# A fused Sinkhorn-attention and feed-forward kernel: a rearranged front, Sinkhorn rounds on GpSimd, and another order of the loads

## The chip, the cores and the metric

The kernel runs on one core of a Trainium2 chip. The metric is device time in microseconds (us) of one execution. A profiled execution is also shown: its span, and who was busy and who waited in it.

## The reference, cut to what matters

Four batches of eight heads, 768 tokens and 64 channels go through an attention whose keys and values are first mixed between eight blocks of 96 tokens. The mixing matrix P comes from five rounds of exponential, row and column normalisation (Sinkhorn). A squared-ReLU feed-forward layer follows.

```python
P = sort_net                                    # (4, 8, 8, 8)
for _ in range(5):
    P = P - np.max(P, axis=-1, keepdims=True)
    P = np.exp(P)
    P = P / (np.sum(P, axis=-1, keepdims=True) + 1e-09)
    P = P / (np.sum(P, axis=-2, keepdims=True) + 1e-09)
k_sorted = np.einsum('bhij,bhjcd->bhicd', P, k_b)   # k, v in 8 blocks of 96 tokens
v_sorted = np.einsum('bhij,bhjcd->bhicd', P, v_b)
scores = scale * np.matmul(q_b, k_sb.transpose(0, 1, 2, 4, 3))   # block i against sorted block i
attn = softmax(scores);  x = np.matmul(attn, v_sb)   # then (3072, 512), heads side by side
h = x @ w_in                                    # 512 x 2048
r = np.maximum(h, 0.0)
out = (s * (r * r) + b) @ w_out                 # 2048 x 512
```

## The kernel before, in words

The order of the instructions on every engine is that of the program text; nothing is rescheduled, and each engine takes its instructions in order. TensorE (PE) does all products and the transposes of batches 0 and 1; VectorE (DVE) and ScalarE (ACT) empty PSUM and do the small arithmetic; GpSimd (POOL) issues the converting loads of q, k, v, `w_in` and `w_out` and rearranges v; SyncE (SP) loads `sort_net` and the f32 values of batch 0, stores the output and issues DMA transposes.

**Front (L76 to L299).** Batch 0 has a Sinkhorn of its own on 128 partitions. The first round comes from an exponential (L240), a product (L250) and a reciprocal (L254). Four rounds follow (loop at L266): an exponential on ACT, a product `rs` on PE, then on DVE a reciprocal, a product with a row sum, and a reciprocal. In every round `permute0` (L209) casts a quarter of the values `v0f`, half on ACT and half on DVE. Between these stand products with zeros, `warm(n, w, m)` (L126), in rounds 0 and 1 `warm(50, 16, 64)`. `pd0` (L258) makes the mixing operand from the last round. POOL meanwhile issues half of the queries, k, all of `w_in`, the other queries and `w_out` (L146 to L166), without waiting for anything but its eight DMA semaphores, each of which must have come back before it is used again.

**First half of batch 0 (L541 to L567).** `kh` and `vh` are 32 small products per piece with `PD0` and an evacuation (A is ACT, D is DVE). `s_piece` makes scores and their exponential, `p_piece` the attention times values and its normalisation on DVE, `t_piece` transposes, `part` begins the first feed-forward product `hps` (L490).

**Feed-forward.** `ffn1(t, slots)` (L494) runs eight pairs of 128 columns of `w_in`; each ends in a ReLU `rt` on ACT (L502) and a square `gt` on DVE (L503), and then in the work that its slot holds. `ffn2(t, slots)` (L508) has a slot after every four products `ops` (L514). There are two of each per batch, t = 2b and 2b + 1. The work on the next batch is in the slots.

**Sinkhorn of batches 1 to 3.** `sink(it)` (L333) does a round on 32 partitions: exponential on ACT, the rest on DVE. Rounds 0, 1, 2 are in slots 3, 5, 7 of `ffn1(1)`, rounds 3 and 4 in slots 0 and 1 of `ffn2(0)`. In slot 2 `build_pd(1)` (L351) takes the result to PE (`pe`, L353) and makes batch 1's mixing operand. `make_bias` (L603, slot 4 of `ffn1(1)`) makes `bias` out of `w_out` with 16 products, four DVE steps, and three copies on POOL (L615). In `ffn2(0)` slots 4, 7 and 9 then hold the keys (`k_piece`), queries (`q_half`) and values (`v_piece`) of batch 1. PSUM is had from two pools, `psa` with three buffers and `psb` with two.

POOL's queue after the front is, in order: memsets, the loads of batch 1, `v_sort(1)` (eight copies, L207), the loads of batch 2, the bias copies, the loads of batch 3, `v_sort(2)` and `v_sort(3)`.

Of the kernel before, what the change touches and what calls it, by code (L numbers as in the profile page):

```python
# [22 lines left out]
def kernel(  # L23
# [49 lines left out]
    CQ = S // 2 // 128  # L73
# [27 lines left out]
    def load_qh(b, half, hs):  # L101
        if b not in QH:
            QH[b] = rawp.tile([128, 2, H, CQ, D], BF, tag="rawq", name="qh")
        qv = q[b].rearrange("h (f p c) d -> f p h (c d)", f=2, c=CQ)
        nc.gpsimd.dma_start(out=QH[b][:, half, hs].rearrange("p h c d -> p h (c d)"),
                            in_=qv[half][:, hs])
# [17 lines left out]
    nc.vector.memset(VP[0][:, :, C2:GAP], 0.0)  # L124

# [20 lines left out]
    load_qh(0, 0, slice(0, 4))  # L146
    load("k", 0, 3)
    load_qh(0, 0, slice(4, 8))
    fill_vs(0)
    load_wi(0, 512, slice(0, 2))  # L150
    load_wi(0, 512, slice(2, 4))
    load_wi(512, 1024)
    load_qh(0, 1, slice(0, 8))
    load_wi(1024, 1536)
    load_wi(1536, 2048)
# [6 lines left out]
    for t, src in ((s_bc, moe_s), (b_bc, moe_b)):  # L162
        nc.gpsimd.dma_start(out=t, in_=src.to_broadcast([128, 1]))
    for c in range(4):
        fs = slice(c * (NF // 4), (c + 1) * (NF // 4))
        nc.gpsimd.dma_start(out=wo[:, fs, :], in_=wov[:, fs, :])  # L166
# [12 lines left out]
    er = const.tile([128, NB], FP)  # L179
    er2 = const.tile([128, NB, 2], FP)  # L180
    bmx = const.tile([128, 2 * NHP, HB, 2], FP)
    ex = const.tile([128, NB], FP)
    rr = const.tile([128, NB], FP)
    csum = const.tile([128, 1], FP)
    crec = const.tile([128, 1], FP)
# [8 lines left out]
                            axis=AX.X, op=ALU.add)  # L194
    nc.vector.tensor_scalar(out=hs64, in0=hs64, scalar1=2.0, scalar2=None, op0=ALU.mult)
    nc.vector.tensor_reduce(out=hsel, in_=ident.rearrange("p (h g) -> p h g", h=H),
                            axis=AX.X, op=ALU.add)
    nc.vector.tensor_reduce(out=nmax, in_=s0, axis=AX.X, op=ALU.max, negate=True)
# [17 lines left out]
    def q_trans(b, half, hp0):  # L216
        if b not in QT:
            QT[b] = trp.tile([128, 2, NHP, CQ, 128], BF, tag="qt", name="qt")
        tr = psb.tile([128, 1024], BF, tag="b", name="tq")
        for a in range(2):  # L220
            for c in range(CQ):
                for e in range(2):
                    o = (a * CQ + c) * 128
                    nc.tensor.transpose(out=tr[e * 64:(e + 1) * 64, o:o + 128],
                                        in_=QH[b][:, half, 2 * (hp0 + a) + e, c, :],
                                        identity=ident)
        return tr

    def q_piece(b, half, hp0, eng):
        tr = q_trans(b, half, hp0)  # L230
        evac(eng, QT[b][:, half, hp0:hp0 + 2],
             tr[:, 0:2 * CQ * 128].rearrange("p (a c t) -> p a c t", a=2, c=CQ))
# [14 lines left out]
    warm(5)  # L247
    warm(16, 16, 64)
# [5 lines left out]
    nc.vector.reciprocal(out=crec, in_=e0[:, 0, NB:NB + 1])  # L254
    src = e0[:, 0, 0:NB]
    PD0 = [const.tile([128, 2, NHP, HB, 2], BF, name=f"pdh{i}") for i in range(2)]
# [8 lines left out]

    for it in range(4):  # L266
        nc.scalar.activation(out=ex, in_=src, func=AF.Exp, scale=crec)
        permute0(it)
        if it == 0:
            nc.vector.tensor_reduce(  # L270
                out=bm.rearrange("p (e a z) -> p e a z", e=2, z=2),
                in_=idv.rearrange("p a e j z -> p e a z j"), axis=AX.X, op=ALU.add)
            nc.vector.tensor_scalar(
                out=bmx, in0=bm.rearrange("p (g z) -> p g z", z=2).unsqueeze(2)
                .broadcast_to([128, 2 * NHP, HB, 2]), scalar1=2.0, scalar2=None, op0=ALU.mult)
# [3 lines left out]
        if it == 3:  # L279
            q_piece(0, 0, 0, "A")  # L280
            warm(2)
        elif it == 2:
            warm(3)
        else:
            warm(50, 16, 64)
        nc.vector.reciprocal(out=rr, in_=rs[:, 0, 0:NB])
        if it < 3:
            nc.vector.scalar_tensor_tensor(out=er, in0=ex, scalar=1.0, in1=rr, op0=ALU.mult,
                                           op1=ALU.mult, accum_out=csum)
        else:  # L290
            nc.vector.scalar_tensor_tensor(
                out=er2, in0=ex.unsqueeze(2).broadcast_to([128, NB, 2]), scalar=1.0,
                in1=rr.unsqueeze(2).broadcast_to([128, NB, 2]), op0=ALU.mult, op1=ALU.mult,
                accum_out=csum)
        nc.vector.reciprocal(out=crec, in_=csum)
        src = er
        if it == 1:
            nc.vector.memset(KS[0][:, :, :, C2:GAP], 0.0)
# [33 lines left out]
    def sink(it):  # L332
        if it == 0:  # L333
            nc.vector.tensor_reduce(out=rstat, in_=sn, axis=AX.X, op=ALU.max)
            nc.vector.tensor_tensor(out=sn, in0=sn, in1=rstat.broadcast_to([BH, NB, NB]),
                                    op=ALU.subtract)
        nc.scalar.activation(out=sn, in_=sn, func=AF.Exp)
        nc.vector.tensor_reduce(out=rstat, in_=sn, axis=AX.X, op=ALU.add)
        nc.vector.reciprocal(out=rrec, in_=rstat)
        nc.vector.tensor_tensor(out=sn, in0=sn, in1=rrec.broadcast_to([BH, NB, NB]), op=ALU.mult)  # L340
        if it == 4:
            return
        nc.vector.tensor_reduce(out=rstat, in_=sn.rearrange("p i j -> p j i"),
                                axis=AX.X, op=ALU.add)
        if it == 0:
            nc.vector.tensor_tensor(out=rstat, in0=rstat, in1=eps, op=ALU.add)
        nc.vector.reciprocal(out=rrec, in_=rstat)
        nc.vector.tensor_tensor(out=sn, in0=sn, in1=spread(rrec, [[0, NB], list(rrec.ap[1])]),
                                op=ALU.mult)
# [21 lines left out]
    def q_half(b, half, eng):  # L371
        if b not in QT:
            QT[b] = trp.tile([128, 2, NHP, CQ, 128], BF, tag="qt", name="qt")
        tr = psa.tile([128, 2, 1024], BF, tag="a", name="tqa")
        for a in range(NHP):
            for c in range(CQ):
                for e in range(2):
                    o = (a % 2 * CQ + c) * 128
                    nc.tensor.transpose(out=tr[e * 64:(e + 1) * 64, a // 2, o:o + 128],
                                        in_=QH[b][:, half, 2 * a + e, c, :], identity=ident)  # L380
        evac(eng, QT[b][:, half].rearrange("p (u a) c t -> p u (a c t)", u=2),
             tr[:, :, 0:2 * CQ * 128])
# [24 lines left out]
    def s_piece(b, half, hp):  # L407
# [3 lines left out]
        for n in range(HB):  # L411
            for e in range(2):
                pr = slice(e * 64, (e + 1) * 64)
                if byp:
                    o = sc[:, e, 0:TG].rearrange("p (c t) -> p c t", c=CQ)[:, :, 32 * n:32 * n + 32]
                    r = QT[b][pr, half, hp, :, 32 * n:32 * n + 32]
# [123 lines left out]

    kh(0, 0, "A", psa)  # L541
    kh(0, 1, "D", psa)
    pd0(1)
    kh(0, 2, "A", psa)
    vh(0, 0, "D", psb)
    vh(0, 1, "A", psb)
    vh(0, 2, "D", psa)
    s_piece(0, 0, 0)
    vh(0, 3, "D", psa)
    q_piece(0, 0, 2, "A")  # L550
    s_piece(0, 0, 1)
    warm(1)
    p_piece(0, 0, 0)
    warm(1)
    p_piece(0, 0, 1)
    t_piece(0, 0, 0, "A")
    s_piece(0, 0, 2)
    part(0, 0, (0,))
    t_piece(0, 0, 1, "D")
    s_piece(0, 0, 3)  # L560
# [3 lines left out]
    p_piece(0, 0, 3)  # L564
    part(0, 1, (0, 1))
    t_piece(0, 0, 2, "A")
# [3 lines left out]
    nc.gpsimd.memset(ones, 1.0)  # L570
    nc.gpsimd.memset(VP[1][:, :, C2:GAP], 0.0)
    nc.gpsimd.memset(KS[1][:, :, :, C2:GAP], 0.0)
    eps = const.tile([BH, NB], FP)
    nc.gpsimd.memset(eps, 1e-9)
    fill_vs(1)
    load("v", 1)
    load("k", 1)
    for half in range(2):
        load_qh(1, half, slice(0, 8))

    def v_sort(b):
        for i in range(8):
            permute(nc.gpsimd, b, RAW["v", b], ds=slice(i * 8, (i + 1) * 8))

    v_sort(1)
    for t in "kv":
        load(t, 2)
    load_q_rows(2)


    rstat = const.tile([BH, NB], FP)
    rrec = const.tile([BH, NB], FP)
# [26 lines left out]
    def QP(hp, eng): return lambda: q_piece(0, 1, hp, eng)  # L619
    def QF(b, half, eng): return lambda: q_half(b, half, eng)  # L620
    def SK(it): return lambda: sink(it)
# [10 lines left out]
    def halves(n, more=()):  # L632

        if n == 1:
            s0 = {0: [SK(3)], 1: [SK(4)], 2: [PDB(1)],
                  4: [K(n, 0, "D"), K(n, 1, "A"), K(n, 2, "D")],
                  7: [QF(n, 0, "D"), QF(n, 1, "A")],
                  9: [V(n, 0, "D"), V(n, 1, "A"), V(n, 2, "D")]}
# [3 lines left out]
        s1 = {0: [V(n, 3, "D"), SC(n, 0, 0), SC(n, 0, 1)],  # L642
# [4 lines left out]
        for i, p in more:  # L647
# [3 lines left out]
    ffn1(0, {0: [KH(1, "D")], 1: [KH(2, "A"), QP(0, "D")],  # L651
             2: [VH(0, "D"), VH(1, "A")], 3: [SC(0, 1, 0), VH(2, "D")],
             4: [VH(3, "D"), SC(0, 1, 1)], 5: [P(0, 1, 0), QP(2, "D")],
             6: [SC(0, 1, 2), P(0, 1, 1), TP(0, 1, 0, "A")],
             7: [SC(0, 1, 3), P(0, 1, 2), TP(0, 1, 1, "D")]}, {0: 2, 1: 2})
# [5 lines left out]
    ffn1(1, {2: [make_sel], 3: [SK(0)], 4: [make_bias], 5: [SK(1)], 7: [SK(2)]}, {0: 2, 1: 2})  # L661
    s0, s1 = halves(1, [(5, LD("k", 3)), (6, LD("v", 3)), (7, lambda: load_q_rows(3))])
# [45 lines left out]
```

## Time and profile before

| | us |
|---|---|
| median of three runs (252.92 to 257.52) | 255.03 |
| the profiled execution | 254.47 |
| its span | 252.3 |
| PE busy in the span | 232.4 (92%) |
| DVE, ACT, POOL busy | 128.7, 97.1, 57.8 |
| first feed-forward product `hps` | at 30.00 |
| `ffn1(1)` runs on from | 57.16 |
| `pe`, PE's product for batch 1's mixing operand | at 75.50 |

Busy time is the time in which an engine executes. A wait is named by the instruction that waits and by the one that released it. The chain of work is followed back from the last instruction: it shows at each moment what the end waited for. In all rows "L" is a line of the kernel before. The granted clock is a record of changes of TensorE's clock; before the first recorded change it is shown as full. The shapes and durations of the products tell more there.

### The profile page before, as it was taken

To read this page: it belongs to the slowest core of one execution; us is meant where nothing else is said; L and a number is where in the kernel's file an instruction comes from. 1 tells how busy PE (TensorE), PEld (TensorE's weight loads), DVE (VectorE), ACT (ScalarE), POOL (GpSimd) and SP (SyncE) were. 2 spreads that over 40 slices of the span, in tenths; PEclk is the share of its full clock that TensorE was granted. 3 is DMA by queue.
4 is the path that set the end of the run, shared out by engine and by line. 5 is a ranking of instruction groups with operands and counts; after the bars stand their busy time and mean duration, and the time that the engine had idled before them with its cause. 6 is when DMAs were issued, how large, how long until landed. Compare 5 with 4: busy or idle time off the path is not lost.

```text
span 252.3 us, 6386 instructions
## 1 busy us (share of the span) xinstructions
PE 232.4 (92%) x2810; PEld 141.6 (56%) x2832; DVE 128.7 (51%) x273; ACT 97.1 (38%) x131; POOL 57.8 (23%) x86
## 2 busy tenths in 40 slices
PE   6997899879919999999999999999999999999994
PEld 3956666545505655565665565656555656664453
DVE  4433454655975479654463566444545674442221
ACT  3433554545511242456640334566403336661000
POOL 8565400992130469900000000000000000000000
PEclk9999999999976999999999999999999999999999
DMA  6999999969901899772001113720021133000122
GB/s 154 263 202 205 152 213 212 151 111 188 85 0 44 159 191 154 107 183 49 0 3 74 53 44 107 191 38 3 3 83 44 44 104 107 0 1 20 65 83 84
DMA packets 42332, 25.07 MB, mean 99 GB/s; under 512 B 33344, under 2 KB 37696, under 8 KB 42304
## 3 DMA queue, kind: packets, MB, share of 16 engines
q0 software_dynamic: 22320, 12.85, 36.6%
q1 hardware_dynamic: 19984, 11.81, 16.6%
q8 instruction: 22, 0.36, 0.6%
q14 instruction: 6, 0.05, 0.1%
HBM read 27.27 MB, written 6.29 MB: 133 GB/s over the span
## 4 chain that ended last, share of the span: by engine, by line
PE 84%; DVE 8%; ACT 3%; issue 3%; DMA 1%; DVEq 0%; ACTq 0%
PE ops L514 31%; PE hps L490 30%; PE pv L442 3%; PE sc L420 3%; PE z L129 3%; PE tv L398 3%; PE vh L323 2%; PE tp L388 2%; DVE gt L503 2%; PE ops L527 1%; PE kh L309 1%; ACT rt L502 1%; DVE x L448 1%; DVE bias L612 1%; PE rs L277 1%
## 5 line engine op out<-in xcount | busy, mean ns | idle before, releaser
L490 PE MATMUL hps<-xt,wi 128*128 128x384 bf16 x512 | 86.6, 326 | 2.5 <-DVE xt L238 1.8
L514 PE MATMUL ops<-wo,gt 128*128 128x512 bf16 x347 | 83.4, 385 | 2.2 <-issue 1.6
L490 PEld LDWEIGHTS <-wi 128*128 128x128 bf16 x512 | 49.1, 98 | 34.8 <-issue 3.3
L502 ACT ACTIVATE rt<-hps 128x768 bf16<-128x768 f32 x64 | 51.7, 810 | 40.4 <-PE hps L490 40.4
L503 DVE TENSOR_TENSOR gt<-rt 128x768 bf16<-128x768 bf16 x64 | 35.9, 561 | 47.4 <-ACT rt L502 47.2
L514 PEld LDWEIGHTS <-gt 128*128 128x128 bf16 x368 | 33.9, 99 | 37.5 <-issue 1.7
L535 DVE SCALAR_TENSOR_TENSOR ot<-ops,s_bc,bias 128x512 f32<-128x512 f32 (+1 forms) x25 | 18.2, 729 | 33.7 <-PE ops L514 31.4
L207 POOL COPY vp<-rawv 128x384 bf16<-128x384 bf16 x24 | 20.1, 888 | 13.0 <-DMA rawv<-in_v_dram 13.0
L448 DVE TENSOR_TENSOR x<-pv,rec 96x512 bf16<-96x512 f32 x32 | 22.0, 687 | 1.1
L428 ACT ACTIVATE at<-sc 112x768 bf16<-112x768 f32 x16 | 12.1, 806 | 21.0 <-PE sc L420 21.0
L424 ACT ACTIVATE at<-sc 112x768 bf16<-112x768 f32 x16 | 12.5, 808 | 12.3 <-PE sc L420 12.3
L442 PEld LDWEIGHTS <-at 112*128 112x128 bf16 (+1 forms) x256 | 13.1, 103 | 7.0 <-ACT at L428 0.6
L116 POOL DMA_DIRECT2D qtok<-in_q_dram x16 | 12.3, 778 | 10.2 <-DMA rawv<-in_v_dram 5.2
L442 PE MATMUL pv<-vs,at 112*128 112x66 bf16 (+1 forms) x256 | 14.3, 198 | 0.0
L238 DVE CAST vs<-tv 112x1024 bf16<-112x1024 f32 x9 | 10.7, 1221 | 5.9 <-PE tv L398 5.9
L129 PE MATMUL z<-zeros 128*64 128x16 bf16 (+1 forms) x127 | 12.4, 238 | 1.4 <-DVE zeros L120 1.2
L447 DVE RECIPROCAL rec<-pv 96x8 f32<-96x8 f32 x32 | 6.4, 201 | 9.4 <-PE pv L442 9.3
L420 PE MATMUL sc<-qt,ks 64*128 64x96 bf16 x256 | 9.2, 208 | 0.9 <-DVE qt L238 0.9
L129 PEld LDWEIGHTS <-zeros 128*64 128x64 bf16 (+1 forms) x128 | 7.9, 155 | 3.5 <-issue 2.1
L236 ACT CAST vs<-tv 112x1024 bf16<-112x1024 f32 x3 | 3.1, 1018 | 16.8 <-PE tv L398 16.8
L323 PE MATMUL vh<-pdh,vp 128*64 128x32 bf16 x256 | 6.7, 199 | 1.8 <-issue 1.8
L238 DVE CAST ks<-tp 128x1024 bf16<-128x1024 f32 x6 | 7.1, 1220 | 1.8 <-PE tp L388 1.6
(108 smaller groups left out, 151.1 us busy)
## 6 DMA issues: line engine op xcount, KB each, us to landing
out_dram<-ot SPq DMA_DIRECT2D x23, 256.0 KB, 2.0
rawv<-in_v_dram POOLq DMA_DIRECT2D x3, 768.0 KB, 11.3
rawk<-in_k_dram POOLq DMA_DIRECT2D x3, 768.0 KB, 6.7
wo<-in_moe_w_out_dram POOLq DMA_DIRECT2D x4, 512.0 KB, 17.1
v0f<-in_v_dram SPq DMA_DIRECT2D x4, 384.0 KB, 5.9
wi<-in_moe_w_in_dram POOLq DMA_DIRECT2D x3, 512.0 KB, 14.5
qtok<-in_q_dram POOLq DMA_DIRECT2D x16, 96.0 KB, 8.1
qh<-in_q_dram POOLq DMA_DIRECT2D x3, 384.0 KB, 19.7
```

Source lines behind the costliest of these rows:

```text
L129: nc.tensor.matmul(out=z[0:m, 0:w], lhsT=zeros[:, 0:m], rhs=zeros[:, 0:w], start=True, stop=True)
L207: eng.tensor_copy(out=o, in_=i)
L238: nc.vector.tensor_copy(out=out, in_=in_)
L420: nc.tensor.matmul(out=o, lhsT=KS[b % 2][pr, g0 + n].rearrange("p z c -> p (z c)"), rhs=r, start=True, stop=True)
L424: nc.scalar.activation(out=at.rearrange("p e (t c) -> p e t c", c=CQ), in_=sc[0:KR, :, 0:TG].rearrange("p e (c t) -> p e t c", c=CQ), func ...
L442: nc.tensor.matmul(out=pv[0:m, e, n * VW:(n + 1) * VW], lhsT=atf[:, c0:c0 + m], rhs=VS[b % 2][:, e * NG + g0 + n, :], start=True, stop=True)
L448: nc.vector.tensor_tensor(out=x[:, :, hp * 128:(hp + 1) * 128].rearrange("p n (e d) -> p e n d", e=2), in0=pvv[:, :, :, 0:D], in1=rec.unsq ...
L490: nc.tensor.matmul(out=H1[t, i][:, f, 0:TG], lhsT=wi[:, hp, fc:fc + 128], rhs=XT[t][:, :, hp, :], start=(hp == 0), stop=(hp == NHP - 1))
L502: nc.scalar.activation(out=rt, in_=h, func=AF.Relu)
L503: nc.vector.tensor_tensor(out=gt[:, 2 * i:2 * i + 2, :], in0=rt, in1=rt, op=ALU.mult)
L514: nc.tensor.matmul(out=ops, lhsT=gt[:, f, m * 128:(m + 1) * 128], rhs=wo[:, f, :], start=(f == 0), stop=(f == NF - 1))
L535: nc.vector.scalar_tensor_tensor(out=ot[:, ns], in0=ops, scalar=s_bc, in1=BIAS[0][:, ns], op0=ALU.mult, op1=ALU.add)
```

## The change

- **Front.** A dummy exponential of one column, on a tile of zeros, is put ahead of ACT's work; the function table is loaded with it. The zero products become `warm(44, 48)` (128 x 128 by 48 columns) ahead of `e0`, `warm(8, 64)` behind it, and two or three products of 512 columns in rounds 0 to 2. The memset of `KS[0]`, `nmax` and `bm` are moved to earlier places on DVE. Each round has its own small tiles (`EXT`, `RRT`, `ERT`, `CST`, `CRT`). Both query transposes of the first half stand in round 3. Behind `pd0` the order becomes values, then keys.
- **Loads.** Queries are loaded as runs of six tokens (64 partitions per half) and transposed as 64 x 64. `w_in`, in pieces of 1024 columns, waits on POOL for a copy of the last `crec`; then come the second half of the queries, `w_in`'s second half, v of batch 1, and `w_out`. k and q of batch 1 are issued in slot 1 of `ffn1(1)`, the loads of batch 2 in slot 0 of `ffn2(0)`.
- **Sinkhorn of batches 1 to 3.** The sums and the normalising products move from DVE to POOL; a sum over eight is three additions (`fold`). Reciprocals stay on DVE, the exponential on ACT. The rounds begin in slots 6 and 7 of `ffn1(0)`, and take two slots each in `ffn1(1)`. `make_bias` goes to slot 7 of `ffn1(1)`, `build_pd(1)` to slot 1 of `ffn2(0)`. `v_sort(1)` is split: four copies ahead of `ffn1(1)`, four in slot 0 of `ffn2(0)`. In `ffn2(0)` values come in slots 5 and 7, keys in 9, queries in 11 and in `ffn2(1)`.

```diff
-    CQ = S // 2 // 128
+    CQ = 6
+    nc.vector.memset(KS[0][:, :, :, C2:GAP], 0.0)
+    dummy = const.tile([128, 1], FP)
+    nc.scalar.activation(out=dummy, in_=zeros[:, 0:1], func=AF.Exp)
...
-    load_qh(0, 0, slice(0, 4))
+    load_qh(0, 0)
     load("k", 0, 3)
-    load_qh(0, 0, slice(4, 8))
     fill_vs(0)
-    load_wi(0, 512, slice(0, 2))
...
+    def load_w():
+        nc.gpsimd.tensor_copy(out=gate, in_=crec)
+        load_wi(0, 1024, slice(0, 2))
+        load_wi(0, 1024, slice(2, 4))
+        load_qh(0, 1)
+        load_wi(1024, 2048, slice(0, 2))
+        load_wi(1024, 2048, slice(2, 4))
+        for t, src in ((s_bc, moe_s), (b_bc, moe_b)):
+            nc.gpsimd.dma_start(out=t, in_=src.to_broadcast([128, 1]))
+        load("v", 1)
+        for c in range(4):
...
-    warm(5)
-    warm(16, 16, 64)
+    warm(44, 48)
...
+    warm(8, 64)
...
         if it == 3:
-            q_piece(0, 0, 0, "A")
-            warm(2)
-        elif it == 2:
-            warm(3)
+            q_ps = [q_trans(0, 0, 0), q_trans(0, 0, 2)]
         else:
-            warm(50, 16, 64)
+            warm(2 if it == 0 else 3)
...
+    load_w()
     pd0(0)
...
+    def fold(x):
+        nc.gpsimd.tensor_tensor(out=st4, in0=x[:, :, 0:4], in1=x[:, :, 4:8], op=ALU.add)
+        nc.gpsimd.tensor_tensor(out=st2, in0=st4[:, :, 0:2], in1=st4[:, :, 2:4], op=ALU.add)
+        nc.gpsimd.tensor_tensor(out=rstat, in0=st2[:, :, 0], in1=st2[:, :, 1], op=ALU.add)
+    def sink_exp():
+        nc.scalar.activation(out=sn, in_=sn, func=AF.Exp)
+        fold(sn)
+    def sink_row(it):
+        nc.vector.reciprocal(out=rrec, in_=rstat)
+        nc.gpsimd.tensor_tensor(out=sn, in0=sn, in1=rrec.broadcast_to([BH, NB, NB]), op=ALU.mult)
+        if it < 4:
+            fold(sn.rearrange("p i j -> p j i"))
         if it == 0:
+            nc.gpsimd.tensor_tensor(out=rstat, in0=rstat, in1=eps, op=ALU.add)
+    def sink_col():
         nc.vector.reciprocal(out=rrec, in_=rstat)
+        nc.gpsimd.tensor_tensor(out=sn, in0=sn, in1=spread(rrec, [[0, NB], list(rrec.ap[1])]),
...
+    q_evac(0, 0, 0, "A", q_ps[0])
+    vh(0, 0, "D", psa)
+    vh(0, 1, "A", psa)
+    pd0(1)
+    vh(0, 2, "D", psa)
+    q_evac(0, 0, 2, "A", q_ps[1])
+    vh(0, 3, "D", psb)
     kh(0, 0, "A", psa)
-    kh(0, 1, "D", psa)
-    pd0(1)
-    kh(0, 2, "A", psa)
+    kh(0, 1, "A", psb)
+    kh(0, 2, "D", psa)
     s_piece(0, 0, 0)
...
-            s0 = {0: [SK(3)], 1: [SK(4)], 2: [PDB(1)],
-                  4: [K(n, 0, "D"), K(n, 1, "A"), K(n, 2, "D")],
-                  7: [QF(n, 0, "D"), QF(n, 1, "A")],
-                  9: [V(n, 0, "D"), V(n, 1, "A"), V(n, 2, "D")]}
+            s0 = {0: [SR(4), lambda: v_sort(1, range(4, 8)), load2], 1: [PDB(1)],
+                  5: [V(n, 0, "D"), V(n, 1, "A")], 7: [V(n, 2, "D"), V(n, 3, "A")],
+                  9: [K(n, 0, "D"), K(n, 1, "A"), K(n, 2, "D")], 11: [QF(n, 0, "A")]}
...
+             2: [VH(1, "A"), QF0(), VH(2, "D")],
...
+             6: [P(0, 1, 1), TP(0, 1, 0, "A"), sink_max],
+             7: [SC(0, 1, 3), P(0, 1, 2), TP(0, 1, 1, "D"), sink_exp]}, {0: 2, 1: 2})
...
-    ffn1(1, {2: [make_sel], 3: [SK(0)], 4: [make_bias], 5: [SK(1)], 7: [SK(2)]}, {0: 2, 1: 2})
-    s0, s1 = halves(1, [(5, LD("k", 3)), (6, LD("v", 3)), (7, lambda: load_q_rows(3))])
+    v_sort(1, range(4))
+    ffn1(1, {0: [SR(0)], 1: [sink_col, sink_exp, load1], 2: [SR(1), make_sel],
+             3: [sink_col, sink_exp], 4: [SR(2)], 5: [sink_col, sink_exp], 6: [SR(3)],
+             7: [sink_col, sink_exp, make_bias]}, {0: 2, 1: 2})
+    s0, s1 = halves(1, [(6, LD("k", 3)), (6, LD("v", 3)), (7, lambda: load_q_rows(3))])
```

## The prediction

> **What bounds the kernel now.** I read the page first, then the busy time by stretches, the chain of work in order of time, and the waits. PE is busy for 92% of the span, so gain is to be looked for where it idles or does products that count for nothing.
>
> ```profile
> PE 232.4 (92%) x2810; PEld 141.6 (56%) x2832; DVE 128.7 (51%) x273; ACT 97.1 (38%) x131; POOL 57.8 (23%) x86
> ...
> PEclk9999999999976999999999999999999999999999
> ```
>
> By stretches (width; busy us of PE, PEld, DVE, ACT, POOL; clock; DMA share; GB/s) one stretch stands out: PE does 4.5 us of 10, at two thirds of the clock.
>
> ```profile
> 60.00:70.00 10.00, 9.87 (x66) 4.97 (x65) 8.00 (x24) 4.92 (x8) 2.24 (x3) 1.00 1.36 104
> 70.00:80.00 10.00, 4.50 (x28) 1.92 (x30) 6.13 (x25) 0.77 (x3) 1.67 (x2) 0.66 0.03 11
> ```
>
> The chain of work (start, us, what) shows why. PE waits for the end of the Sinkhorn, which waited on DVE behind the bias; the products behind `pe` then run at 0.43 us, not 0.217.
>
> ```profile
> 65.35 0.67 DVE bias L609
> 66.05 0.75 DVE bias L612
> 66.82 0.75 DVE bias L612
> 67.60 0.76 DVE bias L612
> ...
> 75.14 0.22 DVE sn L340
> 75.50 0.66 PE pe L353 x2
> 76.15 3.52 PE ops L514 x8
> ```
>
> The same chain in the front: the zero products of rounds 0 and 1 hold up `rs` (2.77 us twice), an unhindered round is the one from 14.60, and "issue" is a wait of PE for nothing that is recorded.
>
> ```profile
> 5.86 0.28 ACT ex L267
> 6.18 0.60 PE rs L277 x2
> 6.78 2.77 PE z L129 x50
> 9.55 0.53 PE rs L277 x2
> 10.07 2.77 PE z L129 x50
> ...
> 14.60 0.31 ACT ex L267
> ...
> 23.14 1.84 issue
> ...
> 30.00 0.48 PE hps L490 x2
> ```
>
> Two more rows: what POOL takes for copies, and when the four loads of `v0f` land after their issue (the last issue is at 3.0).
>
> ```profile
> L615 POOL COPY bias<-bias x3: 608/922/1610, 68.5 to 70.1; 32x512 f32<-32x512 f32 x3
> ...
> DMA to landing us min/median/max: 3.4/5.9/8.7
> ```
>
> **The rounds of the front: 3.4 us earlier, not 4.4.** The table load (1.28) no longer follows `sort_net`, but the memset of `KS[0]` (0.48) now stands ahead of `nmax`: `s0e` goes from 4.00 to 3.2, `ex` from 5.86 to 5.1. Four unhindered rounds (14.60 to the `crec` that ends at 16.29: 1.7) end at 11.9. But on DVE each round's cast of a quarter of v stands ahead of its reciprocal, and the last quarter lands at 3.0 + 8.7 = 11.7; the bytes of q and k that share the engines with it are the same. Cast 0.47, reciprocal 0.21, product 0.26, `crec` 0.17, `pd0` 0.29, gaps: 13.1, against 16.61. So early table and shorter zero products are partly absorbed by this load. The 44 products of 48 columns: rows on either side are 55 ns (16 columns) and 74 ns (66 columns, 8 in 0.59); 44 x 0.074 = 3.2 ends at 4.5, where `e0` is due; at the 0.15 of one 128-column weight load they end at 7.8 and cost up to 2.5 more. I take 0.074. The six-token transposes are 48 small ones in round 3, in PE's wait for DVE: nothing.
>
> **From `pd0` to the first `hps`: 10.6 us instead of 12.8.** Before, it is 17.23 to 30.00. There 96 `kh` products take 2.74 us (28 ns each) at 17.23; at 36.60, 32 of them take 0.68 (21 ns), and 512-column products go from some 0.48 (two zero products in 0.97 at 16.33) to 0.217 later. So PE runs at half speed until about 28, though the clock row says full. If it is at full speed earlier: seven pieces of 0.65 (4.5), last evacuation 0.8, scores 0.35, their exponential 0.91, `pv` 0.5, DVE 0.9, transpose and copy 0.85: 8.8. If not: 11.2 (pieces 0.91). The 1.84 of "issue" may come again at either, as the products before it are as many. Ends: 8.8 and 13.0. I take full speed with the wait, 10.6: the new zero products have 128 x 128 weights, as the zero and `pv` products of the stretch 25 to 28.8 nearly have, behind which PE is fast; `kh` and `vh`, with 64 columns of weights, did not bring that about. First `hps` at 23.8, 6.2 earlier. `w_in`, held back until `crec` (12.9), is issued from 13 on at 0.75 a piece; before, its pieces of 256 KB landed 10.8 after issue (median), behind 1.2 MB of q and k. Now nothing is ahead of them, so 17 to 20 for the first two; their cover is 4 us, and if it is gone, `hps` waits for them.
>
> The Trainium skill ("TensorE: Matmul & The Clock Gate", Part 1) states that one busy window of about 3.4 us releases the clock and one idle window takes it back. The slow row at 76.15 behind an idle stretch agrees; the dense `kh` and `vh` of 17 to 23 us, which stayed slow, do not. By the rule the stretch takes 10.6, by the slow rows of `kh` and `vh` 13.0, and the time is 254.1.
>
> **First `ffn1`: 0.65 earlier again.** The wait of scores for `qt` (0.92 at 48.7) goes, as the queries are ready earlier; 24 more transposes at some 10 ns cost 0.25. The wait for `xt` at 53 stays: DVE's order there is the same. `ffn1(1)` runs from 57.16 - 6.85 = 50.3.
>
> **Sinkhorn on POOL: 21.0 us from there to `pe`, before 18.3.** Counted from the start of `ffn1(1)`:
> - The reciprocal of round 0 stands behind `gt` of slot 0: done at 2.3 (before, that `gt` ends at 59.3, 2.1 after). The exponential, its fold, and four `v_sort` copies (0.84 each) lie ahead and hidden by `ffn1(0)`.
> - POOL's small steps are not in the trace. Bounds: the memset of 32x8, 0.12, and the copy of 384 elements, 0.89. The slope between gives 64 elements 0.23, 8 elements 0.12, plus 0.06 between two steps: I take 0.25 for a product and 0.5 for a fold, that is 0.21 a step.
> - Rest of round 0: product, fold, epsilon, reciprocal (0.2), product, exponential (0.26), 0.08 per hand-over: 2.0, to 4.3.
> - Round 1: on POOL three DMA issues (0.55 + 2 x 0.87) stand between fold and product: 4.6, to 8.9.
> - Rounds 2 and 3: the exponential holds up `rt` (0.81) and `gt` (0.56) of the next slot, and the row's reciprocal stands behind that `gt`, so the first fold is hidden: 0.26 + 1.37 + two reciprocals 0.4, two products 0.5, a fold 0.5, hand-overs 0.4 = 3.45 each, to 15.8. Later `rt` cost PE nothing that counts: it waits at `pe` anyway.
> - The bias follows on DVE the last column reciprocal (15.05): 0.67 + 3 x 0.75, to 18.0. Round 4's reciprocal stands behind it, and on POOL its product stands behind the three bias copies: 2.5 (1.85 to 3.2), to 20.6. Product and hand-overs: `pe` at 21.0.
>
> In the kernel before the copies were off the path; now DVE's 2.95 and POOL's 2.5 lie on it, and by them alone (the bias products of PE done at 11.3) `pe` could not come before 17. `pe` at 50.3 + 21.0 = 71.3, 4.2 earlier than 75.50.
>
> The skill ("GPSIMD Engine Reference", section 3) speaks against this move: elementwise work with two inputs is about half as fast there as on DVE. Twice DVE's 0.21 and 0.15 for these steps would be 7.7 for the 21 steps on the path instead of 4.4, and the time 255.0.
>
> **After `pe`.** It stands in slot 1, not 2: four `ops` more to do, 0.87. 48 more transposes of batch 1: 0.2. PE idles some 8 us instead of 5.6; half speed after it cost (79.97 - 75.5) / 2 = 2.2 and may cost 1.7 to 3.4: 0.3 more. Values and keys change places with their products unchanged. On POOL the loads of batches 2 and 3 come some 20 and 5 us later; k and v of batch 2 are used from 128 on, hidden. SP's queue keeps its order.
>
> **Sum.** -6.2 - 0.65 + 2.7 = -4.2; + 0.87 + 0.2 + 0.3 = -2.8 with rounding. Span 249.5. The profiled execution took 254.47, its span 252.3, so 2.2 lie around it: 251.7, against a median of 255.03.
>
> **The rivals.**
> - *All of the front is kept (faster).* 8.8 instead of 10.6, POOL's steps at their lower end (21 x 0.12 = 2.5 instead of 4.4), copies at 0.61: -1.8 - 1.9 - 0.65: 247.3. For it: POOL's memsets are that short; DVE idles during the copies. Against it: the wait of 1.84.
> - *PE stays slow in the front (no change).* 13.0 instead of 10.6: 254.1. For it: `kh` and `vh` ran dense and slow. Against it: their weights were half an array.
> - *POOL's steps are dear (slower).* At 0.6 a step, 21 x 0.39 = 8.2, and the fold of 1.8 outgrows its cover of 1.37, 0.43 three times: +9.5, 261.2. It decides from 0.56 on. For it: every step is an instruction with a hand-over; against it: the memsets.
> - *A transfer collides.* DMA transposes of x for `ffn1(2)` landed 3.6 after 101.64, 1.8 ahead of use, when loads had ended. The loads of batch 3 would now be under way; behind one (k: 6.7 to landing) the stall is 4.9: 256.6.
>
> **How the numbers follow.** Chances: the sum 0.48, all kept 0.18, slow front 0.14, dear steps 0.14, collision 0.06. A measurement of this kernel tells about 2% from no change, 5.1 us: limits 249.9 and 260.1. The sum's own range is 249 to 254.5, 0.08 of its 0.48 below 249.9. Faster: 0.18 + 0.08 = 0.26; slower: 0.14; between: 0.60. The range reaches from the kept front, 247, to 258, beyond the collision; it leaves out the dear steps and the far ends.
>
> **What would show it.** `pd0` at 13 right behind a cast that waited for v; `hps` at 22 to 26; a wait of POOL's last product for the bias copies, and `pe` 21 us after `ffn1(1)` began, with PE idle for 8. It is wrong if POOL's additions take over 0.5, if `hps` waits for `w_in`, or if the zero products end after `e0` is due.

## The result, and the profile after

The changed kernel takes 266.09 us (median of 4 runs, 264.85 to 267.17), against 256.27 for the kernel before beside it: ratio 1.048, interval 1.037 to 1.058. It is slower, and above the predicted range. Its profiled execution also took 266.09, with a span of 264.3, 12.0 more than before. (Some executions show a lower granted clock and take longer; ratios, and the times in the table of experiments, are of the others.) The kernel before was profiled in its run of 254.47, 1.8 below that median, and its rows are to be read with that.

| us in the span | before | after | change | predicted |
|---|---|---|---|---|
| `pd0` done | 16.6 | 14.5 | -2.1 | -3.5 |
| first `hps` | 30.00 | 28.80 | -1.2 | -6.2 |
| from there until `ffn1(1)` runs on | 27.16 | 29.47 | +2.3 | -0.65 |
| from there to `pe` | 18.34 | 22.70 | +4.4 | +2.7 |
| `pe` to the first `hps` of batch 1 (`ffn1(2)`) | 31.5 | 37.9 | +6.4 | +1.4 |
| from there to the end | 145.4 | 145.5 | 0 | 0 |

In the page, PE is 2.5 us less busy in a span 12 longer, and POOL has 36 instructions more. PE's loss is waiting.

```profile
PE 229.9 (87%) x2840; PEld 138.4 (52%) x2864; DVE 126.7 (48%) x252; ACT 97.9 (37%) x133; POOL 63.4 (24%) x122
...
PEclk9999999999995997999999999999999999999999
```

Stretches of 10 us, columns as in the prediction. The hole of PE (4.50 busy before) is deeper and wider, with a slow clock behind it.

```profile
60.00:70.00 10.00, 7.08 (x44) 4.04 (x42) 3.68 (x13) 3.80 (x7) 6.57 (x21) 1.00 0.44 81
70.00:80.00 10.00, 3.25 (x27) 1.18 (x26) 5.04 (x11) 1.89 (x4) 5.70 (x19) 0.94 0.51 78
80.00:90.00 10.00, 8.87 (x89) 4.26 (x90) 4.30 (x7) 1.02 (x1) 9.66 (x14) 0.72 0.50 83
90.00:100.00 10.00, 7.36 (x223) 5.12 (x225) 4.99 (x5) 3.47 (x3) 2.65 (x4) 1.00 1.59 195
```

The chain of work after, in order of time:

```profile
2.94 10.13 DMA v0f<-in_v_dram
13.09 0.49 DVE vp L214
14.56 3.60 PE vh L325 x128
18.16 2.57 PE kh L311 x96
...
22.11 2.40 issue
...
28.80 0.48 PE hps L506 x2
...
43.55 1.97 issue
...
75.54 0.71 DVE bias L625
76.28 0.75 DVE bias L628
77.05 0.76 DVE bias L628
77.83 0.77 DVE bias L628
78.65 0.60 POOL bias L631
79.29 0.61 POOL bias L631
79.94 0.61 POOL bias L631
80.97 0.68 PE pe L369 x2
81.66 5.53 PE ops L530 x16
...
96.84 0.88 PE tqa L396 x48
97.72 3.26 issue
100.98 0.82 PE ops L530 x3
```

Four things are to be seen. The front waits for the last quarter of v, cast at 13.09 on DVE. The products behind `pd0` still take 28 ns each; the clock's first release, the moment from which its record shows full speed again, is at 27.59. PE has three long waits of the kind "issue": 2.40 among the scores, 1.97 at product 29 of 32 of a `vh` piece, 3.26 behind 48 small query transposes. And the seven bias steps stand in one row ahead of `pe`; the 16 `ops` behind it run at 0.35 us on average.

### The profile page after: what moved, and what is told of

Read it like the earlier page. It is cut to its first block, busy times and chain, and to the rows that moved or that the text cites. A ratio compares the mean times of both kernels' runs of the same rounds, so it can differ in the third digit from the quotient of the medians.

```text
span 264.3 us, 6469 instructions
## 1 busy us (share of the span) xinstructions
PE 229.9 (87%) x2840; PEld 138.4 (52%) x2864; DVE 126.7 (48%) x252; ACT 97.9 (37%) x133; POOL 63.4 (24%) x122
## 4 chain that ended last, share of the span: by engine, by line
PE 77%; issue 6%; DVE 5%; POOL 4%; DMA 4%; ACT 2%; SPq 1%; ACTq 0%; DVEq 0%
PE ops L530 31%; PE hps L506 28%; DMA v0f<-in_v_dram 4%; PE pv L458 3%; PE sc L436 3%; PE tv L414 3%; PE vh L325 2%; PE tp L404 2%; ACT rt L518 2%; PE ops L543 1%; PE kh L311 1%; PE tqa L396 1%; POOL sn L356 1%; DVE gt L519 1%; DVE bias L628 1%
## 5 line engine op out<-in xcount | busy, mean ns | idle before, releaser
L530 PE MATMUL ops<-wo,gt 128*128 128x512 bf16 x346 | 84.5, 389 | 5.7 <-issue 5.2
L519 DVE TENSOR_TENSOR gt<-rt 128x768 bf16<-128x768 bf16 x64 | 38.3, 601 | 47.6 <-ACT rt L518 47.5
L214 POOL COPY vp<-rawv 128x384 bf16<-128x384 bf16 x24 | 18.9, 835 | 0.0
L240 ACT CAST vs<-tv 112x1024 bf16<-112x1024 f32 x4 | 4.1, 1018 | 29.3 <-PE tv L414 29.3
L463 DVE RECIPROCAL rec<-pv 96x8 f32<-96x8 f32 x32 | 6.4, 201 | 13.8 <-PE pv L458 13.8
L242 DVE CAST vs<-tv 112x1024 bf16<-112x1024 f32 x8 | 9.6, 1221 | 4.8 <-PE tv L414 4.8
L436 PEld LDWEIGHTS <-ks 64*128 64x128 bf16 x256 | 6.6, 99 | 5.4 <-issue 4.5
L132 PE MATMUL z<-zeros 128*128 128x48 bf16 (+2 forms) x62 | 7.6, 282 | 1.5 <-DVE zeros L120 1.2
L369 PE MATMUL pe<-sn,emat 32*128 32x64 f32 x6 | 1.8, 394 | 7.6 <-POOL sn L356 7.6
## 6 DMA issues: line engine op xcount, KB each, us to landing
rawv<-in_v_dram POOLq DMA_DIRECT2D x3, 768.0 KB, 11.7
```

The source lines that it names most:

```text
L214: eng.tensor_copy(out=o, in_=i)
L436: nc.tensor.matmul(out=o, lhsT=KS[b % 2][pr, g0 + n].rearrange("p z c -> p (z c)"), rhs=r, start=True, stop=True)
L519: nc.vector.tensor_tensor(out=gt[:, 2 * i:2 * i + 2, :], in0=rt, in1=rt, op=ALU.mult)
L530: nc.tensor.matmul(out=ops, lhsT=gt[:, f, m * 128:(m + 1) * 128], rhs=wo[:, f, :], start=(f == 0), stop=(f == NF - 1))
```

## The experiments

Times in us; the last three columns are times of the span, read from each profile. "Before" for a ratio is the kernel before on the same chip.

| kernel | time | ratio, interval | first `hps` | `pe` | `ffn1(2)` |
|---|---|---|---|---|---|
| `sink_on_dve` | 264.06 | 1.032, 1.023-1.042 | 27.5 | 79.0 | 116.4 |
| `bias_late` | 269.44 | 1.054, 1.046-1.062 | 28.5 | 78.0 | 122.0 |
| `loads_early` | 266.82 | 1.048, 1.039-1.056 | 29.9 | 88.7 | 122.4 |
| `old_tail` | 260.42 | 1.019, 1.010-1.027 | 29.65 | 79.9 | 113.4 |
| `three_token` | 261.14 | 1.022, 1.014-1.030 | 24.8 | 75.5 | 112.3 |
| `dense_zeros` | 259.23 | 1.013, 1.004-1.022 | - | - | - |
| `before_short_front` | 252.39 | 0.988, 0.981-0.996 | 27.3 | 74.6 | 106.6 |
| `before_front_bias` | 250.50 | 0.979, 0.973-0.985 | 26.1 | 70.8 | 104.05 |
| `three_token_old_tail` | 252.30 | 0.988, 0.980-0.996 | 25.1 | 73.6 | 105.2 |
| `three_token_tail_bias` | 249.66 | 0.980, 0.968-0.993 | 25.1 | 70.0 | 102.0 |
| `tail_bias_no_hold` | 247.98 | 0.972, 0.966-0.978 | 26.2 | 68.6 | 100.6 |
| `tail_bias_dense` | 246.00 | 0.964, 0.955-0.973 | 22.4 | 67.4 | 99.45 |

**Sinkhorn on DVE, in the new slots** (`sink_on_dve`)

```diff
-        nc.gpsimd.tensor_tensor(out=st4, ...)
-        nc.gpsimd.tensor_tensor(out=st2, ...)
-        nc.gpsimd.tensor_tensor(out=rstat, ...)
+        nc.vector.tensor_reduce(out=rstat, in_=x, axis=AX.X, op=ALU.add)
...
-        nc.gpsimd.tensor_tensor(out=sn, ...)
+        nc.vector.tensor_tensor(out=sn, ...)
```

> The changed kernel with the sums and products of the later Sinkhorns back on VectorE, in the same slots; all else as changed. Theory (GpSimd's small steps, and what stands between them on its queue, are on the path): rounds of 3.0 us instead of 3.95, no load issues (2.0) and no bias copies (1.9) between the steps, so `pe` comes about 15 us after the start of `ffn1(1)` instead of 22.7, TensorE idles 2 us there instead of 7.6, and the time falls from 266 by 8 to 10, to 256 to 258. Rival (the loss sits in TensorE's waits for nothing recorded, and in the loads that are now late): `pe` may come earlier, but the stretch from `pe` to the next `ffn1` stays 38 us, and the time falls by no more than the 7.6 of idle: 259 to 264.

A round took 3.03 instead of 3.95, and `pe` came 17.7 behind the start of `ffn1(1)` instead of 22.7: what stood on POOL had 5.0 of the path. The theory had `pe` at 15, and PE idling 2 ahead of it; it idled 5.3. Of the 266.09 only 2.0 went: PE's clock was released only at 34.4 here (27.6 in the changed kernel), `ffn1(1)` began 3.0 later, and `pe` to `ffn1(2)` stayed at 37.4. (The loads of batch 1 also left POOL's freer queue at 39.7 instead of 64.3, so the run moves them as well.) The step has its direction, and the total is the rival's.

**The bias behind the mixing operand** (`bias_late`)

```diff
-             7: [sink_col, sink_exp, make_bias]}
+             7: [sink_col, sink_exp]}
...
-1: [PDB(1)],
+1: [PDB(1)], 2: [make_bias],
```

> The changed kernel with the bias made in slot 2 of `ffn2(0)`, behind batch 1's mixing operand, instead of slot 7 of `ffn1(1)`. Theory (the last reciprocal waits on VectorE for the bias, and the last product on GpSimd for its copies): `pe` comes 3.2 us earlier after the start of `ffn1(1)`, 19.5 instead of 22.7; the time falls by about 3, to 263. Rival (the path is held elsewhere, the bias is hidden): `pe` at 22 to 23 after the start, time 266.

`pe` came 19.5 behind `ffn1(1)`, 3.2 sooner. But POOL's queue now holds four copies of `v_sort` and the load issues ahead of the bias copies, which ran at 93.7 to 95.6. The first outputs need `bias`, they hold the PSUM buffers, and PE waits for them:

```profile
PE ops L530 <- DVE ot L551: 6.2, 1, 6.2
```

(Waits of this kernel: who waited for whom, total us, times, longest.) The 3.2 gained ahead of `pe` were lost twice over behind it: `pe` to `ffn1(2)` took 44.0 for 37.9.

**The loads of batches 1 and 2 early, as before** (`loads_early`)

```diff
+    load1()
+    load2()
...
-    ffn1(1, {0: [SR(0)], 1: [sink_col, sink_exp, load1], ...
+    ffn1(1, {0: [SR(0)], 1: [sink_col, sink_exp], ...
```

(called ahead of `ffn1(0)`; `load2` leaves slot 0 of `ffn2(0)`)

> The changed kernel with the loads of k and q of batch 1 and all loads of batch 2 issued right behind the memsets of the front, ahead of the Sinkhorn, instead of in slot 1 of `ffn1(1)` and slot 0 of `ffn2(0)`. Theory (late loads cost twice: 2.0 us of issue between two Sinkhorn steps on GpSimd, and company for TensorE's instruction fetch after `pe`): `pe` 20.7 after the start of `ffn1(1)`, the unexplained wait of 3.3 us behind the query transposes of batch 1 goes or shrinks below 1, the stretch from `pe` to the next `ffn1` falls from 38.0 to 34, the time to 260. Rival (the wait comes from the denser instruction stream, whatever is loaded): the wait of about 3 stays and only the 2.0 of issue go: 264.

The 3.26 behind the transposes is gone, and `pe` to `ffn1(2)` is 33.7, as expected. (Its chain ends on a DMA transpose of x that landed 6.27 after its issue; PE waited only 0.80 for it.) Ahead of `pe` all of it was lost, since the issues sit on the queue that does the Sinkhorn: `pe` came 26.7 behind `ffn1(1)`, not 20.7. The chain around 64: POOL is stuck among the issues until the buffers and earlier loads are free, and the first exponential's fold, the four `v_sort` copies and the first normalising product (69.41; at 60.59 in the changed kernel) come behind it:

```profile
41.13 23.27 DMA rawv<-in_v_dram
64.40 0.28 issue
64.69 0.77 POOL qtok L116
65.46 0.06 issue
65.52 0.24 POOL st L341
...
66.32 3.09 POOL vp L214 x4
69.41 0.58 POOL sn L356
```

**Only the front** (`old_tail`: Sinkhorn, slots and loads of batches 1 to 3 as before, but v of batch 1 still issued ahead of `w_out`)

```diff
-    ffn1(1, {0: [SR(0)], 1: [sink_col, sink_exp, load1], ...
+    ffn1(1, {2: [make_sel], 3: [SK(0)], 4: [make_bias], 5: [SK(1)], 7: [SK(2)]}, ...
-            s0 = {0: [SR(4), lambda: v_sort(1, range(4, 8)), load2], 1: [PDB(1)], ...
+            s0 = {0: [SK(3)], 1: [SK(4)], 2: [PDB(1)], ...
```

> The changed front with its loads, together with the Sinkhorn, the slots of `ffn1(1)` and `ffn2(0)`, the bias and the loads of batches 1 and 2 as in the kernel before. Theory (the front and its loads come out even, the loss is in the later Sinkhorns and what was moved around them): 254 to 257, the time of the kernel before within 1%. Rival (the front's order of loads and the doubled transposes carry a good part of it): 259 or more.

The rival holds: the front, on which the forecast's gain rested, is a loss of 1.9% by itself (1.0 to 2.7); `ffn1(1)` began at 61.5. Its chain has the wait, the 28 ns products behind `pd0`, and a slow `hps` (0.80 the pair):

```profile
14.45 3.60 PE vh L325 x128
18.04 2.57 PE kh L311 x96
...
21.99 2.98 issue
...
29.66 0.80 PE hps L495 x2
```

**Query loads and transposes of three tokens again** (`three_token`)

```diff
-    CQ = 6
+    CQ = S // 2 // 128
...
-            QH[b] = rawp.tile([128, H, CQ, D], ...
+            QH[b] = rawp.tile([128, 2, H, CQ, D], ...
-                                        in_=QH[b][pr, 2 * (hp0 + a) + e, c, :],
-                                        identity=ident[pr, pr])
+                                        in_=QH[b][:, half, 2 * (hp0 + a) + e, c, :],
+                                        identity=ident)
```

> The changed kernel with the query loads and transposes of batches 0 and 1 as before: runs of three tokens on 128 partitions, half as many transposes of 128 x 64. Theory (the six-token load is the cause of the later end of v's load, and the doubled transposes run TensorE into its waits sooner): the last quarter of v lands at 11.7 instead of 13.1, `pd0` at 13 instead of 14.2, and the two waits for nothing recorded in the front (2.4 to 3.0 and 2.0 in all runs of this front) shrink together by 1 or more; time 263. Rival (the waits come at a fixed place of the instruction stream, whatever the transposes; the load of v is late for other reasons): waits of 4 to 5 us in all stay, `pd0` at 14, time 265 to 267.

The waits of 2.40 and 1.97 are gone, v's last quarter is there 2.8 earlier (10.26 for 13.07), `hps` comes 4.0 and `ffn1(1)`, at 52.45, 5.8 earlier. So is the 3.26 behind the query transposes of batch 1, though its loads are as late as in the changed kernel. Of all this, 4.9 reach the end. With `pe` earlier, the DMA transposes of x are under way together with the loads of batch 3 and PE waits for them, the prediction's fourth rival at nearly its price (4.9):

```profile
PE hps L504 <- DMA xt<-x: 4.3, 1, 4.3
```

**Zero products of 512 columns in the changed front** (`dense_zeros`)

```diff
-    warm(44, 48)
+    warm(7)
...
-            warm(2 if it == 0 else 3)
+            warm((3, 6, 3)[it])
```

> The changed kernel with zero products that fill TensorE's waits in the front: 7 of 512 columns ahead of `e0` instead of 44 of 48, and 3, 6, 3 of 512 columns in rounds 0 to 2 instead of 2, 3, 3. Theory (TensorE runs at half speed in the front for want of full products; 48 columns were too few): the `kh` products behind `pd0` take 20 ns instead of 28, the first feed-forward product comes 2 us earlier, `ffn1(1)` starts at 55 to 57, the time is 261 to 263. Rival (the products between, with half the columns or with waits, decide, and the zeros do not reach that far): 28 ns, first feed-forward product at 28 to 30, time 265 to 267.

Open in itself: two runs gave some 259, two 264; the profile is of one of 264, and its rows are not used. `tail_bias_dense` below asks the same of another kernel.

**The kernel before, with the early table load and short zero products alone** (`before_short_front`)

```diff
+    dummy = const.tile([128, 1], FP)
+    nc.scalar.activation(out=dummy, in_=zeros[:, 0:1], func=AF.Exp)
...
-            warm(50, 16, 64)
+            warm(2 if it == 0 else 3)
```

> The kernel before with two parts of the change alone: the early exponential, so that the function table is loaded early, and two or three zero products of 512 columns in rounds 0 and 1 instead of fifty of 16. Theory (both shorten the rounds, up to the load of v, which here lands at 11.7): `pd0` at 13 instead of 16.3, the first feed-forward product at 27 instead of 30.0, time 253 to 254 beside 256.3 of the kernel before. Rival (TensorE's waits for its instructions and the half speed take it back, as in the changed kernel): first feed-forward product at 29 or later, 255 to 258.

The first `hps` is the theory's, and the time 0.6 below its range. `pd0` is not: it was done at 14.75, since v's last quarter landed at 12.99 here, with the loads of the kernel before, whose own profile has it at 11.66. The 1.2% are 3.0 us; between the two profiles 2.7 are seen at the first `hps` and 0.4 at `ffn1(2)`.

**The same, with the bias behind the mixing operand** (`before_front_bias`: `make_bias` from slot 4 of `ffn1(1)` to slot 2 of `ffn2(0)`, behind `PDB(1)`)

> As the run with the early exponential and the short zero products on the kernel before, and the bias made in slot 2 of `ffn2(0)`, behind batch 1's mixing operand, where VectorE has no Sinkhorn step left and GpSimd's copies come ahead of the loads of batch 3. Theory (the bias holds up the Sinkhorn on VectorE by its 2.95 us there): `pe` 15 to 15.5 us after the start of `ffn1(1)` instead of 18.3, TensorE idles 2.5 instead of 5.6 and keeps its clock; another 3 to 5 us: 249 to 251. Rival (the bias is done in a wait of the Sinkhorn, or the first store now waits for it): as without it, within 1.

`pe` came 15.2 behind `ffn1(1)` instead of 18.4, and the time fell by 1.9 (2.4 by the ratios). Here POOL's copies have nothing ahead of them, so the move that cost 3 in `bias_late` gains.

**The changed front with three-token loads and the old rest** (`three_token_old_tail`: the edits of `three_token` and `old_tail` together)

> The changed front with the loads and transposes of three tokens (128 partitions) again, and the Sinkhorn, its slots and the loads of batches 1 to 3 as before. It tells whether the six-token loads are the whole loss of the front, apart from everything behind it. Theory (of the front's loss, the six-token form is the main part): first hps at 24.8 as in three_token (old_tail: 29.65), ffn1(1) from 52.5 to 55 (61.5), pe 18.3 behind that, the rest as in old_tail: 251 to 254. Rival (the loss is elsewhere in the front, in the clock or w_in held back): ffn1(1) at 58 or later, 257 to 260.

Against `old_tail` the six-token form alone, load and transposes together, is worth 8.1. `ffn1(1)` began at 55.28, `pe` 18.3 behind it. Without it the front is worth 1.2% against before (0.4 to 2.0), no more than the two parts of `before_short_front`. Of a gain of 4.9 at the first `hps`, 1.8 is left at `ffn1(2)` in the profiles: the clock was released for 3.4 us at 13.4, was then at half again from 16.8, and full only from 33.9, against 28.6 in the kernel before.

**The same with the bias behind the mixing operand** (`three_token_tail_bias`)

> The same, with the bias behind the mixing operand of batch 1, as in before_front_bias. Theory: pe 15.2 behind the start of ffn1(1), 3 less than in three_token_old_tail, and the time 248 to 251. Rival: the earlier pe finds the next wait (the clock, or batch 1's keys) and nothing is gained: 251 to 254.

As the theory has it: 15.2 behind `ffn1(1)`, and 2.6 less.

**That kernel with zero products of 512 columns, and that kernel with `w_in` not held back** (`tail_bias_dense`: the edit of `dense_zeros`; `tail_bias_no_hold`: the copy of `crec` into `gate` goes)

> three_token_tail_bias, with zero products of 512 columns in the front (7 ahead of e0, 3, 6, 3 in the rounds) as in dense_zeros. In three_token_tail_bias the clock is released only at 32.8, as the products of 25 to 32 (hps pairs at 0.80) show, and the front's 4.9 us at the first hps shrink to 3.7 at the first ops. Theory (the late release is what eats the rest of the front's gain): release at some 10, kept now that the waits for issue are gone; vh and kh 17 ns each, hps at 23, ops 2 earlier, 247 to 248.5. Rival (dense zeros only delay the rounds, and the clock is lost again in the small products, as it was in dense_zeros): 249 to 252.

> three_token_tail_bias without the wait of w_in for crec: its pieces are issued right behind k. It tells what holding back does by itself. Theory (it keeps the engines free for v, whose last quarter sets the last round: 10.4 with the hold): v's last quarter lands after 12, pd0 after 13.5 instead of 12.3, first hps and the time 1 to 2 later, 250.5 to 252. Rival (the hold is needless): v lands as before, w_in and with it v of batch 1 earlier, 248.5 to 250.

For the dense products the theory holds: they give 3.7 (the two intervals overlap), in the fastest kernel of all, 3.6% below the kernel before. The clock record shows the release at 9.7, and half speed from 37.0 to 40.4 and from 67.7 to 71.1. Its chain:

```profile
1.20 3.17 PE z L132 x7
...
8.00 2.20 PE z L132 x6
...
12.93 2.20 PE vh L324 x128
15.13 0.57 PE kh L310 x34
15.70 1.06 issue
16.75 1.18 PE kh L310 x62
...
22.41 0.48 PE hps L493 x2
...
34.03 1.68 issue
```

128 products take 2.20 (17 ns) for the 3.60 of `three_token_tail_bias`. The theory of the hold falls: without it v's last quarter lands at 9.92 as with it (9.85), and the time is not longer but 1.7 lower; these intervals overlap as well, and the release came at 25.4 for 32.8.

## Why the prediction was wrong, step by step

- **Rounds of the front: mis-sized by 1.4.** The shape was right: `pd0` stands behind a cast that waited for v. What failed is "the last quarter lands at ... 11.7; the bytes of q and k that share the engines with it are the same": it landed at 13.07. In the five kernels with the changed front and six-token queries it came at 11.1 to 13.2, in the five with three-token queries at 9.7 to 10.3. The 44 zero products took 1.94 (44 ns each, 74 predicted; the 74 is from eight products in 0.59, which counts the last one to its end, while they start some 55 ns apart). `w_in`'s first two pieces landed at 21.8 and 26.0, not 17 to 20, but the first `hps` waited for `xt`, not for them.
- **`pd0` to the first `hps`: the step that failed most, 14.2 for 10.6,** outside its own ends. "The new zero products have 128 x 128 weights", so full speed, is refuted: the products behind them took 28 ns. The seven pieces took 6.2 for the 4.5 of full speed, and waits of 2.40 and 0.33 stood in place of 1.84; that is 2.6 of the 3.6, and the zero products among the scores, 1.5 in the chain, which the list of terms leaves out, cover the rest. (The slow stretch of 11.2 is not the sum of its listed terms either: with pieces of 0.91 they make 10.7.) The rival of the slow front was the true course here, at 14.2 for its 13.0.
- **"The six-token transposes ... nothing": wrong, and the costliest line.** They were costed by PE's busy time, nothing in round 3 and 0.25 and 0.2 later. The six-token form taken out is worth 8.1 in front of the old tail (260.42 to 252.30) and 4.9 in front of the new one: v earlier, the waits of 2.98 and 1.97 nearly gone, and what follows them. Load and transposes went back in one run, so how the 8.1 divide between them is not shown.
- **First `ffn1`: sign wrong, +2.3 for -0.65.** Waits of 0.38 and 1.97 at `vh`, for which nothing stood in the sum, are the whole of it; PE is as busy as before (23.87 for 23.76). The 0.92 for `qt` went, as predicted, but the other waits grew by as much.
- **Sinkhorn on POOL: direction right, 22.7 for 21.0.** Bias and copies took 5.4 from their first step to `pe` (5.95 predicted). The rounds ahead were the mis-sized term: the bias began 17.3 behind `ffn1(1)`, not 15.05, and a round took 3.95 for 3.45. A fold took 0.8 with its gaps, not 0.5, and a product beside DVE's `gt` 0.65, not 0.25. POOL's row, in order of time:

```profile
69.87 0.65 POOL L356 TENSOR_TENSOR sn<-sn,rrec 32x64 f32<-32x64 f32 x1 [0.60 <-DVE rrec L355]
70.60 0.29 POOL L341 TENSOR_TENSOR st<-sn 32x32 f32<-32x32 f32 x1
70.97 0.21 POOL L342 TENSOR_TENSOR st<-st 32x16 f32<-32x16 f32 x1
71.25 0.19 POOL L343 TENSOR_TENSOR rstat<-st 32x8 f32<-32x8 f32 x1
71.75 0.31 POOL L364 TENSOR_TENSOR sn<-sn,rrec 32x64 f32<-32x64 f32 x1 [0.30 <-DVE rrec L363]
```

  From the product at 69.87 to the end of the fold at 71.44 is 1.57 for four steps, 0.39 each with gaps: below the 0.56 from which the rival of dear steps decides, but not the memsets' price. The rule that the Trainium skill has for it ("GPSIMD Engine Reference", section 3), twice DVE's time, would have made the stage 24.3 by the prediction's 7.7 (21.0 + 7.7 - 4.4); the measured 22.7 lies between it and the prediction's slope. (The prediction does not give its count for the 7.7; eight products and thirteen additions at twice 0.21 and 0.15 make 7.3, and the stage 23.9.)
- **After `pe`: +6.4 for +1.4.** "On POOL the loads of batches 2 and 3 come some 20 and 5 us later; ... hidden" is the failed step. Those of batch 3 came 16.5 later (`rawk` issued at 98.25 for 81.71). Hidden they are as data. But PE waited 3.26 and 0.33, and after that its clock was at half for a second time, from 102.68 to 106.09; that costs 1.7, an estimate (half of the 3.41). With the predicted 0.87 and 0.2 and with the half speed behind `pe` (until 85.61, 0.1 more than before) the sum is 6.5. In these kernels the wait stood only where two things met, as three stretches at or behind the query transposes of batch 1 show: the changed kernel, `loads_early` and `three_token` (columns as in the prediction, the last two the DMA engines' share and GB/s):

```profile
97.70:101.00 3.30, 0.04 (x3) 0.07 (x3) 0.00 (x0) 1.44 (x1) 1.11 (x2) 1.00 2.31 178
104.90:108.00 3.10, 3.10 (x74) 1.78 (x72) 0.96 (x1) 2.35 (x3) 0.92 (x2) 1.00 0.96 196
90.60:92.40 1.80, 1.80 (x31) 1.05 (x32) 0.75 (x1) 0.92 (x1) 0.77 (x1) 1.00 2.38 158
```

  PE stood still with the many small packets of the q rows of batch 2 (share 2.31; from 95 to 102 us 6210 of 6460 packets are under 512 bytes) and 48 transposes in a half. It did not with the same 48 among the larger packets of batch 3 (0.96), nor with 24 among the small packets (2.38). `sink_on_dve` has both, a share of 2.39 and a wait of 2.43. How the one hinders the other is not shown.
- **The collision.** The prediction has the transposes of x issued at 101.64 land 3.6 later, 1.8 ahead of use. 3.6 is the median of six; these took 4.86 and landed 0.5 ahead of use. In the changed kernel nothing waited for them, but in `three_token` PE did, for 4.3.
- **The sum.** The front in the changed form costs 4.2 (`old_tail` to 256.27; 4.8 by its ratio), and the rest 5.7 (266.09 to 260.42). Undoing the six-token form and the rest together gives 13.8, and what stays, `three_token_old_tail`, is 1.2% faster than before. But `before_short_front`, with the early table load and the short zero products alone, is 1.2% faster too, and with the bias moved behind `pe` the two are alike again (0.979 and 0.980). So these two parts are sound; that the rest of the new front gains anything is not shown. The step from 3.4 and 2.2 to 6.2 at the first `hps` holds another 0.6 that the prediction does not name: before, PE began `kh` only 0.6 after `pd0`, and now begins `vh` at once.

What stays open: what sets off PE's "issue" waits. In the five kernels with the changed front and six-token queries whose rows are used, one stands at the same second `sc` of the front (2.4 to 3.0), and in four of them another at `vh` (2.0 to 2.2). With half as many transposes they are 0.3 to 1.3, elsewhere, but for one of 1.7 at `vh` with dense zeros; the kernel before has one of 1.84. So the number of transposes bears on them but does not explain them. In the trace of the changed kernel a 16 KB packet of the instruction queue starts within 1 us of the start of each (22.1, 43.2, 98.6), and took 0.95 to 1.02 as elsewhere; whether it is late in being asked for was not tried.

## What to carry to other kernels

Cost a split step by how many instructions it issues on a dense engine and by what its transfer takes from others, not by its busy time alone: the six-token queries, with twice the transposes, stood in the sum with 0.45 us and were worth 5 to 8. Try the parts of a large change singly: two small parts of this front gave the same 1.2% as all of it with three-token queries. Before a chain of small steps goes to an engine that also issues loads, read what that queue waits for; the load and the chain then take turns at hurting each other. And where an engine idles ahead of a late result, look for work put on that result's own path: the bias behind the mixing operand gave 2 to 3 us, but only with its queue free.

## What the runs showed of the hardware

- The record of the granted clock shows full speed from the start of the span, while the same `vh` product takes 28 ns up to the first release and 17 behind 512-column zero products. The Trainium skill ("TensorE: Matmul & The Clock Gate", Part 1) has one dense window release the clock. In the changed kernel 44 products of 48 columns (1.94) and 6.2 of dense `vh` and `kh` did not; in `tail_bias_dense` seven of 512 columns (3.17) and those of the rounds did, by 9.7.
- Dense `vh` and `kh` kept a clock once released in `tail_bias_dense` (full speed to 37.0, over a wait of 1.06 among them). In `three_token_old_tail` it was lost at 16.8, with a wait of 0.80 among them.
- The same products do not always bring the same release. In `three_token` and `three_token_old_tail` PE's products up to 13.3 are the same, and their times agree to some 0.1 us; the first was released at 24.1, the second at 13.4 for a first time. Their first 128 `vh` products:

```profile
12.73 3.59 PE L324 MATMUL vh<-pdh,vp 128*64 128x32 bf16 x128
12.62 2.50 PE L324 MATMUL vh<-pdh,vp 128*64 128x32 bf16 x128
```

  The other two with three-token loads and the changed kernel's zero products were released at 25.4 and 32.8. In all records, the stretches between two changes are multiples of 3.41 us.
- A POOL product of 32 x 64 takes 0.31 alone and 0.65 beside DVE's `gt` (69.81 to 70.37), a two-input step on bf16; a bias copy of 32 x 512 took 0.61 with DVE idle, up to 1.61 before.
